# The last row of an output weight in two transfers by partitions, and fifteen tiny transfers behind it

## The chip, the cores and the metric

The kernel runs on one core of one Trainium2 chip. The metric is device time in microseconds (us) of one execution; the time before is the median of three runs. The trace is of one profiled execution, and its times are counted from the first instruction.

## What is computed

One decode step for two tokens of width 512, gated by a small MLP. Cut to what matters:

```python
x  = A_x                                      # (2, 1, 512)
xn = layernorm(x)
q  = (xn @ wq)                                # 32 heads of 128
p  = softmax(q . k_cache / sqrt(128))         # 2 x 32 heads x 8192 keys
o  = p @ v_cache                              # two caches of 268 MB each
s  = o.reshape(2, 1, 4096) @ wo               # wo: 4096 x 512, 8 MB
g  = silu(gelu(layernorm(xn) @ w1 + b1) @ w2 + b2)
return x + s * g
```

## The kernel before

The two caches are read in 32 steps of two heads each (`N = 32`); a step's keys are 8 MB, 64 KB on each of 128 partitions, and so are its values. Keys go to one of two buffers `kb`, values to the one buffer `vb`. In each step VectorE multiplies the keys by the query and sums (lines 555 and 562), ScalarE takes the exponentials (line 583), and TensorE (PE) weighs the values (line 606). The values of the last step go in two halves into a `kb` buffer, so that `vb` is free for `wo`.

All transfers are issued by SyncE (SP), in the order in which `load` (line 328) is called in the program, on one hardware queue. SP waits before an issue only until the destination's earlier users are done. A small planner (`Plan`) records every operation with what it reads and writes and puts the waits in: a transfer has a semaphore named by its third argument, which rises by 16 when the transfer has landed, and whoever reads its key waits for it. Transfers with the same name share one semaphore. A reader of several of them waits for the count of the last, that is for all.

The weight `wo` is viewed as 128 partitions by 32 rows `c` of 512 columns (`wo_r`), where partition p holds the 32 rows 32p to 32p + 31 of the matrix. It is loaded in seven pieces behind the last values: the rows `c` 0-15, 16-23, 24-28, 29, 30, and the last, 31, in two, columns 0-383 and 384-511. They are called wo0 to wo6 here, after their semaphores. The pieces are cut in lines 340 to 342 and loaded in lines 651 to 654:

```python
    for i, (a, e) in enumerate(((0, CUT), (CUT, D)), len(WO_PIECES) - 2):
        load(wo_sb[:, OC - 1, a:e], wo_r[:, OC - 1, a:e], f"wo{i}", [("wo", i)], over=["vb"])
```

When the last step's values are weighed and normalised (`on`), PE multiplies by `wo`, row by row as the pieces land: rows 0 to 23 in line 683, rows 24 to 28 in line 696, whose sum `acc` VectorE copies to `early` (line 698), and the rows 29, 30 and 31 in line 704, each in sixteen chunks of 32 columns (`chunks`), which is 32 instructions of PE, since each 32-bit matmul is two. Between row 30 and row 31 line 712 adds `early` in. `piece(c, n)` names the key of the piece that a chunk waits for. A scan on VectorE (line 718) multiplies by the gate and adds x, and SP issues the output (line 721), 112 rows of 256 bytes. The program ends when that has landed.

Of the kernel before, what the change touches and what calls it, by code (L numbers as in the profile page):

```python
# [21 lines left out]
class Plan:  # L22
# [18 lines left out]
    def op(self, eng, fn, r=(), w=(), over=(), it=None, loop=False, dma=None):  # L41


        o = Op()
        o.eng, o.fn, o.it, o.loop, o.dma, o.tell = eng, fn, it, loop, dma, False
        need = {}

        def after(d, war):
            if d.dma is None and dma is None and d.eng == eng and (eng == "pe" or war):
                return  # L50
            if d.dma is None:
                if need.get(d.eng) is None or need[d.eng].idx < d.idx:
                    need[d.eng] = d
            else:
                k = ("dma", d.dma)
                if need.get(k) is None or need[k].idx < d.idx:
                    need[k] = d

        for k in r:
            if k in self.writer:  # L60
                after(self.writer[k], False)
        for k in list(w) + list(over):
            if k in self.writer:
                after(self.writer[k], False)
            for d in self.readers.get(k, ()):
                after(d, True)
        clock = self.clock[eng]
        need = {k: d for k, d in need.items() if clock.get(k, 0) < d.idx}
        o.deps = [(k, d) for k, d in need.items()
                  if not any(e is not d and e.done.get(k, 0) >= d.idx for e in need.values())]  # L70
        for _, d in o.deps:
            for k, v in d.done.items():
                clock[k] = max(clock.get(k, 0), v)
        own = eng if dma is None else ("dma", dma)
        self.count[own] = o.idx = self.count.get(own, 0) + 1
        o.done = dict(clock)
        o.done[own] = o.idx
        for k in w:
            self.writer[k] = o
            self.readers[k] = []  # L80
        for k in r:
            if k not in w:
                self.readers.setdefault(k, []).append(o)
        self.ops.append(o)
# [80 lines left out]
def decode_kernel(nc, x, kc, vc, wq, wo, w1, b1, w2, b2, out):  # L165
# [20 lines left out]
    OC = DH // PH  # L186
    QS = 4
    CH = QT * QS
    CW = D // CH
# [11 lines left out]
    op = plan.op  # L201

    def pe(fn, r=(), w=(), it=None, loop=False):
        op("pe", fn, r, w, it=it, loop=loop)
# [10 lines left out]
    def sbuf(name, shape):  # L215
        return nc.alloc_sbuf_tensor(name, shape, F32).ap()

    def psum(name, shape):
        return nc.alloc_psum_tensor(name, shape, F32).ap()
# [5 lines left out]
    vb = sbuf("vb", [P, KP * DH])  # L225
# [3 lines left out]
    wo_sb = vb.rearrange("p (c n) -> p c n", c=OC)  # L229
# [9 lines left out]
    blk = sbuf("blk", [P, QT])  # L239

    pick = sbuf("pick", [B, P])

    b2w = sbuf("b2w", [P, R])

# [5 lines left out]
    res = sbuf("res", [P, CW, 2])  # L250
# [18 lines left out]
    onp = sbuf("onp", [P, LAST, 2 * CM - RM])  # L269
# [43 lines left out]
    wide = psum("wide", [P, D])  # L313
# [4 lines left out]
    def bank():  # L318
        i = turn[0] % 4
        turn[0] += 1  # L320
        return scratch[i], f"s{i}"
# [6 lines left out]
    def load(dst, src, sem, w, over=()):  # L328
        op("sp", lambda: nc.sync.dma_start(dst, src), (), w, over=over, dma=sem)
# [10 lines left out]
    WO_PIECES = (0, 16, 24, 29, 30, 31, 32)  # L340
    WIDE = WO_PIECES[-5]
    CUT = D - P


    load(w1_sb, w1.rearrange("(p c) f -> p c f", p=P), "w1", ["w1"])
# [54 lines left out]
    for c in range(QT):  # L400
        dve(lambda c=c: nc.vector.memset(b2w[R:R + 1, (QT * B + B) * c:(QT * B + B) * c + B], 1.0), ["b2w"], ["b2w"])
    dve(lambda: nc.vector.tensor_reduce(
        out=slot, in_=ident.rearrange("p (g r) -> p g r", r=R)[:, :, :CM].rearrange("p g (s b) -> p s g b", b=B),
# [103 lines left out]
    for i in range(NQ):  # L507
        for c in range(ND):
            wv = wq_sb[:, c, :].rearrange("p (h s d) -> p h s d", s=U, d=DH)
            a = (NQ - 1 - i) * B  # L510
# [8 lines left out]
    for k in range(N // NB):  # L519

        b, e = divmod(k, HH // NB)
        i, g = divmod(e, GQ)
        p, kp = bank()
        for s in range(U):
            a = R * (U * g + s) + B * i + b
# [124 lines left out]
    wo_r = wo.rearrange("(p c) n -> p c n", p=P)  # L650
    for i, (a, e) in enumerate(zip(WO_PIECES[:-1], WO_PIECES[1:-1])):
        load(wo_sb[:, a:e], wo_r[:, a:e], f"wo{i}", [("wo", i)], over=["vb"])
    for i, (a, e) in enumerate(((0, CUT), (CUT, D)), len(WO_PIECES) - 2):
        load(wo_sb[:, OC - 1, a:e], wo_r[:, OC - 1, a:e], f"wo{i}", [("wo", i)], over=["vb"])

    max_dve(N - 1)
    exps(N - 1)
# [19 lines left out]
    def piece(c, n=0):  # L677
        return ("wo", max(i for i, a in enumerate(WO_PIECES[:-1]) if a <= c) + int(c == OC - 1 and n >= CUT))

# [21 lines left out]
    def chunks(c, lo, hi):  # L701
        for q in range(lo, hi):
            g, sl = q % QT, q // QT
            pe(lambda c=c, q=q, g=g, sl=sl: matmul(
                sums[R * g:R * g + CM, :, 0], onp[:, c - (OC - LAST), CM - RM - RM * sl:2 * CM - RM - RM * sl],
                wo_sb[:, c, q * CW:(q + 1) * CW], start=(c == OC - LAST and sl == 0), stop=(c == OC - 1 and q >= CH - QT)),
               ["onp", piece(c, q * CW), "o4", "wide_x"], ["wide"])

    for c in range(OC - LAST, OC - 1):
        chunks(c, 0, CH)  # L710
    for g in range(QT):
        pe(lambda g=g: matmul(sums[R * g:R * g + CM, :, 0], to_own,
                              early[:, g * CW:(g + 1) * CW], start=False, stop=False),
           ["to_own", "early"], ["wide"])
    chunks(OC - 1, 0, CUT // CW)
    chunks(OC - 1, CUT // CW, CH)

    dve(lambda: nc.vector.tensor_tensor_scan(
        out=res.rearrange("p n k -> p (n k)"), data0=gate.rearrange("p n k -> p (n k)"), data1=wide[:, :2 * CW],
        initial=0.0, op0=ALU.mult, op1=ALU.add), ["wide", "wide_x"] + [("gate", j) for j in range(QT)], ["res"])  # L720
    op("sp", lambda: nc.sync.dma_start(out, res[:ROWS].rearrange("p n k -> p (n k)")), ["res"], dma="out")

    plan.emit(HEADS)

# [2 lines left out]
ROWS, COLS, TOKENS, BLOCK, SLOTS = 112, 64, 2, 32, 4  # L727
# [24 lines left out]
```

## Time and profile before

| | before |
|---|---|
| median of three runs | 1298.91 us (1298.90 to 1299.01) |
| span of the profiled execution, first to last instruction | 1297.6 us |
| time of the median outside that span | 1.3 us |
| DMA queue busy, share of 16 engines | 99.7% |
| read from HBM | 559.30 MB, 431 GB/s over the span |
| VectorE busy | 1138.0 us (88%) |
| PE busy | 407.6 us (31%) |

No time of the profiled execution other than its span is on record. A row such as `1267.28 26.18 DMA vb<-in_A_wo_dram` says at which time a piece of work began and how many us it took. A landing is the time of issue and the us to landing that the profile gives with it. "x32" is a count of instructions; PE's own work (PE) and its weight loads (PEld) have rows of their own, and a weight load begins where its matmul's waits are over. DMA share is the busy share of the 16 DMA engines in a stretch; a packet is one contiguous piece that an engine moves, or the write that reports a finished transfer.

### The profile page before, as it was taken

How to read it: one execution, taken by the hardware profiler on the slowest of the kernel's cores; microseconds unless marked ns; L12 is line 12 of the kernel's file. 1: busy time of each engine (PE TensorE's matmuls, PEld its weight loads, DVE VectorE, ACT ScalarE, POOL GpSimd, SP SyncE). 2: the span in 40 equal slices, each digit the busy share in tenths (PEclk: the TensorE clock that was granted, in tenths of full speed). 3: DMA queues.
4: the chain of work that ended last, by engine and by line, in shares of the span. 5: the costliest groups of instructions: out<-in, count | busy, mean ns of one | idle time of the engine just before them, and what ended most of it. 6: DMA issues, size and time to landing. Idle time of an engine off the chain costs nothing.

```text
span 1297.6 us, 6944 instructions
## 1 busy us (share of the span) xinstructions
PE 407.6 (31%) x2796; PEld 123.4 (10%) x2796; DVE 1138.0 (88%) x294; ACT 78.0 (6%) x250; POOL 1.4 (0%) x8
## 2 busy tenths in 40 slices
PE   5703333312333312333311333321333321233328
PEld 1100110000101000101100101100001100001103
DVE  3599999988889988889988888988888988888991
ACT  1200000000000000000000000000000000000000
POOL 0000000000000000000000000000000000000000
PEclk9856666556666656666656666656666655666658
DMA  9999999999999999999999999999999999999998
GB/s 404 445 425 440 428 432 438 426 444 424 434 438 424 446 424 440 430 426 444 426 438 430 430 440 426 444 424 434 438 424 446 424 432 438 424 446 426 425 433 372
DMA packets 11231, 559.42 MB, mean 431 GB/s; under 512 B 1364, under 2 KB 1620, under 8 KB 1880
## 3 DMA queue, kind: packets, MB, share of 16 engines
q1 hardware_dynamic: 11224, 559.33, 99.7%
q8 instruction: 4, 0.07, 0.0%
q14 instruction: 3, 0.02, 0.0%
HBM read 559.30 MB, written 0.03 MB: 431 GB/s over the span
## 4 chain that ended last, share of the span: by engine, by line
DMA 71%; PE 24%; DVE 3%; issue 1%; ACT 0%; SPq 0%; DVEq 0%
DMA vb<-in_A_v_cache_dram 68%; PE po L606 22%; DMA vb<-in_A_wo_dram 2%; DVE kb L555 1%; DVE sc L562 1%; PE s L433 1%; DMA vb<-in_A_x_dram 1%; PE po L513 1%; PE s L479 0%; PE s L435 0%; DVE vb L441 0%; DVE vb L380 0%; ACT L454 0%; PE acc L696 0%; PE s L486 0%
## 5 line engine op out<-in xcount | busy, mean ns | idle before, releaser
L555 DVE TENSOR_TENSOR kb<-kb,Q 128x8192 f32<-128x8192 f32 x64 | 555.5, 8681 | 99.6 <-DMA kb<-in_A_k_cache_dram 93.1
L562 DVE TENSOR_REDUCE sc<-kb 128x64 f32<-128x8192 f32 x64 | 552.3, 8666 | 0.0
L606 PE MATMUL po<-vb,PZ 128*8 128x512 f32 x1984 | 282.3, 733 | 286.1 <-DMA vb<-in_A_v_cache_dram 284.8
L578 PE MATMUL s<-nm,srow 1*128 1x2 f32 x64 | 18.6, 358 | 360.8 <-DVE nm L572 360.8
L606 PEld LDWEIGHTS po<-vb,PZ 128*8 128x8 f32 x1984 | 56.3, 103 | 485.9 <-issue 482.4
L569 PE MATMUL s<-ident,mx 128*1 128x128 f32 x32 | 11.8, 369 | 197.8 <-DVE mx L566 197.8
L578 PEld LDWEIGHTS s<-nm,srow 1*128 1x128 f32 x64 | 15.9, 306 | 370.1 <-DVE nm L572 370.1
L613 ACT COPY o<-po 128x512 f32<-128x512 f32 x32 | 18.8, 586 | 528.2 <-PE po L606 528.2
L579 ACT COPY bias<-s 128x2 f32<-128x2 f32 x32 | 5.1, 160 | 623.9 <-PE s L578 623.9
L615 PE MATMUL s<-mod,o 128*128 128x2 f32 x256 | 33.6, 253 | 22.1 <-ACT o L613 22.1
L615 PEld LDWEIGHTS s<-mod,o 128*128 128x128 f32 x256 | 31.1, 191 | 51.4 <-ACT o L613 51.4
L583 ACT ACTIVATE PZ<-sc,bias 64x128 f32<-64x128 f32 x64 | 25.5, 399 | 1.8
L569 PEld LDWEIGHTS s<-ident,mx 128*1 128x1 f32 x32 | 2.5, 79 | 201.4 <-DVE mx L566 170.8
L621 DVE TENSOR_TENSOR Z<-blk,s 128x8 f32 (+1 forms) x32 | 5.2, 163 | 13.3 <-PE s L615 13.3
L441 DVE COPY vb<-vb 2x384 f32<-2x384 f32 x4 | 1.8, 499 | 15.4 <-ACT vb L437 15.4
L433 PE MATMUL s<-vb 128*2 128x512 f32 (+1 forms) x24 | 12.1, 654 | 0.3 <-ACT vb L393 0.3
L583 ACT ACTIVATION_READ_ACCUMULATOR PZ<-sc,bias 64x1 f32 x64 | 11.8, 185 | 0.0
L566 DVE TENSOR_REDUCE mx<-sc 128x1 f32<-128x128 f32 x32 | 9.2, 286 | 1.1
L587 ACT ACTIVATE ZR<-half,rs 128x8 f32 (+1 forms) x32 | 9.6, 301 | 4.1
L606 PE MATMUL po<-kb,PZ 128*8 128x512 f32 x64 | 9.4, 754 | 1.4 <-ACT PZ L583 1.4
L572 DVE TENSOR_REDUCE nm<-s 1x2 f32<-1x128 f32 x32 | 8.7, 272 | 0.3 <-PE s L569 0.3
L688 DVE COPY wide<-x 128x32 f32<-128x32 f32 x1 | 0.2, 195 | 9.0 <-ACT o L686 9.0
(101 smaller groups left out, 90.3 us busy)
## 6 DMA issues: line engine op xcount, KB each, us to landing
kb<-in_A_k_cache_dram SPq DMA_DIRECT2D x4, 4096.0 KB, 42.9
kb<-in_A_v_cache_dram SPq DMA_DIRECT2D x2, 4096.0 KB, 40.9
vb<-in_B_w_dram SPq DMA_DIRECT2D x2, 2752.0 KB, 12.1
vb<-in_A_wo_dram SPq DMA_DIRECT2D x1, 4096.0 KB, 19.0
vb<-in_A_wo_dram SPq DMA_DIRECT2D x1, 2048.0 KB, 23.6
vb<-in_A_wo_dram SPq DMA_DIRECT2D x1, 1280.0 KB, 26.2
vb<-in_A_wo_dram SPq DMA_DIRECT2D x2, 256.0 KB, 26.3
vb<-in_A_v_cache_dram SPq DMA_DIRECT2D x31, 29.5
```

The source lines that it names most:

```text
L433: pe(lambda f=f, w=w, ph=ph, c=c: matmul(ph[:B, :w], yT[:, c, :], w1_sb[:, c, f:f + w], start=(c == 0), stop=False), ["yT", "w1"], [k])
L513: pe(lambda i=i, c=c, wv=wv, a=a, j=j, hd=hd: matmul(PO[R * j:R * j + NQ * B, :].rearrange("m (h d) -> m h d", d=DH), xnT[:, c, a:a + NQ * ...
L555: vector(n, n, lambda n: nc.vector.tensor_tensor(out=k, in0=k, in1=cols(Q, n * DH, DH).unsqueeze(1).to_broadcast([P, M, DH]), op=ALU.mult) ...
L562: vector(n, n, lambda n: nc.vector.tensor_reduce(out=SC[:, s * M:(s + 1) * M], in_=k, axis=AX.X, op=ALU.add), [("kb", i, s)], [("sc", s)])
L566: vector(n, n, lambda n: nc.vector.tensor_reduce(out=MX, in_=SC, axis=AX.X, op=ALU.max), [("sc", 0), ("sc", 1)], ["mx"])
L569: pe(lambda i: transpose(PM[:1, :P], MX, ident), ["mx", "ident"], ["s1"], it=n, loop=n > 0)
L578: pe(lambda i: matmul(PN[:, :U], srow, NM, start=True, stop=True), ["srow", "nm"], ["s2"], **one)
L583: act(lambda i, r=r, s=s: nc.scalar.activation(PZ[r, :, s, :], sc[r], AF.Exp, bias=BIAS[r, s:s + 1], scale=SCALE, accum_out=RS[r]), ["bias ...
L587: act(lambda i: nc.scalar.activation(cols(ZR, i * UP - UP, UP), half, AF.Copy, scale=RS), ["half"] + [("rs", s) for s in range(U)], [("ZR" ...
L606: pe(lambda i, t=t, j=j, v=v: matmul(PO[R * j:R * j + U * JW, :], PZ[:, t].rearrange("p s j -> p (s j)"), v[:, t * JW:(t + 1) * JW, :].rea ...
L613: act(lambda i: nc.scalar.copy(O4, PO), ["po"], ["o4"], **one)
L615: pe(lambda i, k=k: matmul(PT[:, :U], O4[:, k * DH:(k + 1) * DH], mod[:, k:U * JW:JW], start=(k == 0), stop=(k == JW - 1)), ["o4", "mod"], ...
```

## The change

The last row of `wo` is loaded by four transfers in place of two: for each of its two column ranges one for the partitions 0 to 119 and one, with a semaphore of its own, for the partitions 120 to 127. The chunks of row 31 wait for both transfers of their range. Behind them SP issues fifteen more transfers, of fifteen rows, fourteen, and so on down to one, each row 32 numbers (128 bytes) of row 0 of `wo`, into a tile `mark` that no instruction reads. They share the semaphore `mark`, and the output waits for all of them.

```diff
+    mark = sbuf("mark", [16, 512])
...
+    MAIN = 120
...
     for i, (a, e) in enumerate(((0, CUT), (CUT, D)), len(WO_PIECES) - 2):
-        load(wo_sb[:, OC - 1, a:e], wo_r[:, OC - 1, a:e], f"wo{i}", [("wo", i)], over=["vb"])
+        load(wo_sb[:MAIN, OC - 1, a:e], wo_r[:MAIN, OC - 1, a:e], f"wo{i}", [("wo", i)], over=["vb"])
+        load(wo_sb[MAIN:, OC - 1, a:e], wo_r[MAIN:, OC - 1, a:e], f"wo{i}r", [("wo", i, "rest")], over=["vb"])
+
+    for k in range(15, 0, -1):
+        load(mark[:k, 32 * k:32 * k + 32], wo_r[:k, 0, :32], "mark", [("mark", k)])
...
-               ["onp", piece(c, q * CW), "o4", "wide_x"], ["wide"])
+               ["onp", piece(c, q * CW), "o4", "wide_x"] + ([piece(c, q * CW) + ("rest",)] if c == OC - 1 else []),
+               ["wide"])
...
-    op("sp", lambda: nc.sync.dma_start(out, res[:ROWS].rearrange("p n k -> p (n k)")), ["res"], dma="out")
+    op("sp", lambda: nc.sync.dma_start(out, res[:ROWS].rearrange("p n k -> p (n k)")), ["res"] + [("mark", k) for k in range(1, 16)], dma="out")
```

## Rows read from the trace of the kernel before

**Rows 1.** The page: the DMA queue, what was read, and the chain that ended last.

```profile
q1 hardware_dynamic: 11224, 559.33, 99.7%
HBM read 559.30 MB, written 0.03 MB: 431 GB/s over the span
DMA 71%; PE 24%; DVE 3%; issue 1%; ACT 0%; SPq 0%; DVEq 0%
```

**Rows 2.** The chain that ended last, end of the span: start us, us, what.

```profile
1267.28 26.18 DMA vb<-in_A_wo_dram
1293.46 0.04 issue
1293.51 1.28 PE acc L696 x40
1294.78 0.56 PE wide L704 x64
1295.35 0.10 PE wide L712 x8
1295.44 0.34 PE wide L704 x32
1295.78 0.02 issue
1295.80 0.29 DVE res L718
```

**Rows 3.** Issues on SP in order of time: start us, us, engine, line, what.

```profile
1226.95 6.42 SPq L329 DMA_DIRECT2D kb<-in_A_v_cache_dram  x2
1266.44 3.44 SPq L329 DMA_DIRECT2D vb<-in_A_wo_dram  x7
...
1267.76 0.43 SPq L329 DMA_DIRECT2D vb<-in_A_wo_dram  x1
...
1268.60 0.33 SPq L329 DMA_DIRECT2D vb<-in_A_wo_dram  x1
...
1268.98 0.90 SPq L329 DMA_DIRECT2D vb<-in_A_wo_dram  x2
...
1269.45 0.43 SPq L329 DMA_DIRECT2D vb<-in_A_wo_dram  x1
```

**Rows 4.** DMA issues: KB each, us to landing (256.0 KB: wo3, then wo4).

```profile
kb<-in_A_v_cache_dram SPq DMA_DIRECT2D x2, 4096.0 KB, 40.9
...
vb<-in_A_wo_dram SPq DMA_DIRECT2D x1, 256.0 KB, 26.4
...
vb<-in_A_wo_dram SPq DMA_DIRECT2D x1, 256.0 KB, 26.2
...
vb<-in_A_wo_dram SPq DMA_DIRECT2D x1, 192.0 KB, 26.3
vb<-in_A_wo_dram SPq DMA_DIRECT2D x1, 64.0 KB, 26.0
out_dram<-res SPq DMA_DIRECT2D x1, 28.0 KB, 1.4
```

**Rows 5.** Line 704's weight loads begun by the stretch's end, in brackets (first: 1294.50).

```profile
1290.00:1294.84 4.84, 0.35 (x32) 1.00 0.83 320
1290.00:1294.87 4.87, 0.38 (x33) 1.00 0.82 318
1290.00:1295.13 5.13, 0.64 (x64) 1.00 0.78 302
1290.00:1295.29 5.29, 0.73 (x65) 1.00 0.76 293
1290.00:1295.44 5.44, 0.88 (x88) 1.00 0.74 285
1290.00:1295.47 5.47, 0.91 (x89) 1.00 0.74 283
```

**Rows 6.** The end in order of time: start us, us, engine, line, what [idle before].

```profile
1294.85 0.29 DVE L698 COPY early<-acc 128x128 f32<-128x128 f32 x1 [1.67 <-PE acc L696]
1295.19 0.12 PEld L712 LDWEIGHTS wide<-early,to_own 128*8 128x8 f32 x8
1296.12 0.35 SPq L721 DMA_DIRECT2D out_dram<-res  x1
```

**Rows 7.** Stretches of the end: busy time by engine, PE clock, DMA share, GB/s.

```profile
1293.50:1294.00 0.50, 0.49 (x20) 0.48 (x24) 0.00 (x0) 0.00 (x0) 0.00 (x0) 1.00 0.62 209
1294.00:1294.60 0.60, 0.60 (x32) 0.59 (x24) 0.00 (x0) 0.00 (x0) 0.00 (x0) 1.00 0.38 118
1294.60:1295.00 0.40, 0.40 (x54) 0.40 (x45) 0.15 (x1) 0.00 (x0) 0.00 (x0) 1.00 0.14 44
1295.00:1296.00 1.00, 0.71 (x77) 0.58 (x66) 0.34 (x2) 0.00 (x0) 0.00 (x0) 1.00 0.00 0
```

**Rows 8.** Packets of 1294.6 to 1295.0; left from 1294.9 on; from 1294.95 on.

```profile
DMA packets 31, 0.02 MB, mean 44 GB/s; under 512 B 5, under 2 KB 31, under 8 KB 31
...
DMA packets 134, 0.03 MB, mean 10 GB/s; under 512 B 130, under 2 KB 134, under 8 KB 134
...
DMA packets 130, 0.03 MB, mean 10 GB/s; under 512 B 129, under 2 KB 130, under 8 KB 130
```

**Rows 9.** Packets of 1296.5 to 1297.6 (the output); of the first 12 us.

```profile
DMA packets 128, 0.03 MB, mean 26 GB/s; under 512 B 128, under 2 KB 128, under 8 KB 128
...
DMA packets 210, 4.19 MB, mean 349 GB/s; under 512 B 18, under 2 KB 18, under 8 KB 20
```

**Rows 10.** What SP waited for before the output: us in total, times, longest.

```profile
SPq L721 <- DVE res L718: 26.2, 1, 26.2
```

## The prediction

> **What bounds the kernel now.** I read the page first. The one hardware DMA queue is busy for 99.7% of the time of its sixteen engines, and the chain that ended last is 71% DMA and 24% PE [rows 1]. For most of the span the kernel is a stream from HBM, and the change touches nothing of that stream: all it edits is issued after the last V chunk. So I read the end only.
>
> The chain of the end [rows 2] says: the third wo piece (wo2, columns 24 to 28) lands at 1293.46, then PE works without a gap until 1295.78, the scan takes 0.29, the output is issued. That is too coarse, because a PE that still drains a matmul counts as busy. I therefore put three views side by side. SP issues the seven wo pieces from 1266.44 on, the last at 1269.45 [rows 3]; with the time to landing of each [rows 4] the landings are wo2 1293.46, wo3 1267.76 + 26.4 = 1294.16, wo4 1268.60 + 26.2 = 1294.80, wo5 1268.98 + 26.3 = 1295.28, wo6 1269.45 + 26.0 = 1295.45. The counts of weight loads at line 704 that had begun by a given time [rows 5] show where PE waits: column 29 needs wo3 and begins at 1294.5, column 30 begins at 1294.87, after wo4, and has all 64 begun at 1295.13. The eight of line 712 follow at 1295.19, behind the copy of `acc` that ends at 1295.14 [rows 6]. The last row of wo, column 31, begins at 1295.29, right at the landing of wo5, and its last eight loads (columns 384 to 511, wo6) begin at 1295.47, right behind wo6. So the last row is in truth bound by the landing of wo5 and wo6, but hardly: 32 loads take (1295.13 - 1294.87) / 31 = 8.4 ns each at best, the eight of line 712 are issued by 1295.24, so without any wait column 31 could start at about 1295.245. The wait on wo5 is worth 0.045 us, and that on wo6 0.02 us, in which matmuls issued earlier still drain. Nothing else in the last 4 us can be given back by this change.
>
> Where do wo5 and wo6 lose time? The DMA share falls step by step, 0.62 over 1293.5 to 1294.0, 0.38 to 1294.6, 0.14 to 1295.0, then 0 [rows 7]. The engines thus finish one after another: what is left after 1293.5 is 0.62 x 0.5 + 0.38 x 0.6 + 0.14 x 0.4 = 0.59 us per engine in the mean, so a mean engine ends at about 1294.1 and the last at 1294.97. In the last stretch 31 packets are left, at 1294.95 two (130 less the 128 of the output, [rows 8, 9]).
>
> **The change part by part.** (a) *The last row by 120 and 8 partitions.* If the 120 partitions go to fifteen engines by eight rows, one engine loses its 16 packets of the last row (8 of 1,536 bytes, 8 of 512), and eight engines get one more row of each transfer. One packet in the tail takes 0.14 x 16 x 0.40 us / 31 = 29 ns [rows 7, 8], so the one engine saves about 16 x 29 = 0.46 us with its two completions some 0.5, and eight others get 2 rows and 2 completions, 0.12 us, more. If the spared engine is the single last one, wo5 and wo6 land earlier by what parts it from the next. At 1294.9 six packets with two completions among them are still left (134 and 130 less the output's 128, [rows 8, 9]), so a second engine was then still at work, less than 0.1 us ahead. Gain on the PE path: between 0 and the 0.065 us that PE waits at all. If a last engine is one of those that get a ninth row: a loss of up to 0.12 us. I take 0.
>
> The trace shows for 112 partitions sixteen completions beside the 112 rows (128 packets, the output) and at the start 18 packets below 512 bytes, which I read as 16 completions of w1 and 2 of x with its two rows [rows 9]; no transfer of 120 rows is in it. [...] No row here tells engines apart.
>
> (b) *Two more waits on PE*, before the first and the thirteenth chunk of column 31. Where column 30 waits for a piece that has landed, the step from load 32 to load 33 is 0.03 us against 0.01 between others [rows 5]: 0.02 us for each wait that is already satisfied, 0.04 us in all. It is on the path; behind it stand the last 32 matmuls, the scan and the output. Bounds 0 and 0.04; I take 0.04, which eats the gain of (a).
>
> (c) *Seventeen more DMA issues on SP.* Seven take 3.44 us [rows 3], 0.49 each; 24 take 11.8 us and end near 1278.2. SP has nothing else until the output: it waits 26.2 us there for the scan [rows 10], so 18 us of cover are left. Cost 0. If that cover were gone, each issue late would cost 0.47.
>
> (d) *The fifteen marks.* They lie behind the wo pieces on the queue, and the output (line 721) now waits for all of them as well as for the scan. Nothing but the output stands behind that wait on SP. Before, the output is issued at 1296.12 [rows 6]. A transfer's last packet precedes its landing by 1295.45 - 1294.97 = 0.48 us. [...] Lower price of a mark: two packets of 29 ns, 0.058 us. Upper price: the 0.17 us from the landing of wo5 to that of wo6, which holds eight rows and a completion. A mean engine with fifteen marks then ends at 1294.1 + 0.12 + 0.87 = 1295.09, landed 1295.57, hidden with 0.55 us to spare; the last engine, were it the one with fifteen, at 1295.96, landed 1296.44, 0.3 us too late. At the upper price these are 1297.25 and 1298.12: the output late by 1.1 and 2.0 us. A row of 128 bytes is nearer to a packet than to eight, so I take the lower price, and for the unknown place of the late engines half of the 0.3: 0.15 us.
>
> **Sum.** (a) 0, (b) +0.04, (c) 0, (d) +0.15: +0.19 us on the span of 1297.6. The median of the runs, 1298.91, lies 1.31 us above that span, and I keep this: 1298.91 + 0.19 = 1299.1. Differences of 0.2%, 2.6 us, are about what a measurement of this kernel can tell from no change, so this is no change.
>
> **The rivals.**
> *Marks in single file.* If each mark is begun only when the one before is written and acknowledged, each costs what the output needs from the end of its issue to landing, 1.4 - 0.35 = 1.05 us [rows 4, 6]. The engine with fifteen would end at 1294.2 + 15 x 1.05 = 1309.95, landed 1310.4, the output 14.3 us late: 1313.2, slower. It decides from 0.27 us a mark on ((1296.12 + 2.6 - 0.48 - 1294.2) / 15). Against it: wo5 and wo6 land only 0.17 us apart with eight rows between. Chance 3%. [...]
>
> *The 120 rows don't spread.* On eight engines (15 rows each) an engine gets 30 packets in place of 16: 14 x 29 ns = 0.4 us, at worst on the last one: 1299.5, still no change. On one engine: 240 packets x 29 ns = 7.0 us behind a mean engine's 1294.1 less its 0.5, landed near 1301.1 against 1295.45: +5.6, 1304.7, slower. For it speaks only that 120 is no power of two; against it that 112 rows made sixteen completions. Chances 5% and 2%.
>
> *The queue holds only so many transfers.* At most nine are in flight in the trace of before: seven wo pieces and two halves of the last V, issued from 1226.95 on with 40.9 us to landing [rows 3, 4]. If sixteen were the limit, the last marks would be issued only as wo5 and wo6 land, the last near 1296.2, landed near 1297.6: the output 1.5 us late, 1300.6, no change (4%). If nine or ten were, some ten marks would be issued after 1295.28 at 0.47 each, the last landed near 1301.4: 5.3 us late, 1304.4, slower (2%).
>
> *Faster.* All of the wait on the late engine is 0.065 us and the whole stretch from wo2's landing to the scan is 2.3 us; 0.2% would need more than this. Only a shift of the stream before, for which the diff has no cause, could give it: 3%.
>
> **How the numbers follow.** The forecast with its bounds (0 to 2.0 us late, or 0.07 earlier) holds 81%, together with the two rivals that stay within 0.2% (5% and 4%) 90%; slower 7%; faster 3%. The range goes from 1298.6 (the whole wait gained, and the 0.1 us by which the runs differ, twice) to 1301.0 (upper price of a mark on the last engine, 2.0 us).
>
> **What would show it.** In the changed profile: 24 wo and mark issues on SP, ended by about 1278; wo2 landing within 0.1 us of 27 us after the first wo issue; column 31 begun at 0.05 us or less behind line 712; the fifteen marks as 120 more packets below 512 bytes with 120 completions more, done within about 1 us of the last wo row; the output issued 0.03 us behind the scan, or up to 0.35 later, and then with SP's wait at line 721 put down to a mark. An output held by 2 us or more behind the scan, or column 31 a microsecond or more behind column 30, would make the prediction wrong.

## The result, and the profile after

| | before | after |
|---|---|---|
| median of the runs | 1298.91 us (20 runs, 1298.76 to 1299.22) | 1301.09 us (20 runs, 1300.80 to 1301.60) |
| ratio, 95% interval | | 1.0017 (1.0010 to 1.0023) |
| span of the profiled execution | 1297.6 us | 1299.6 us |
| scan begins | 1295.80 | 1296.67 |
| output issued | 1296.12 | 1298.10 |
| packets, of them below 512 bytes | 11231, 1364 | 11485, 1618 |

The median is 2.18 us later. That is within the 0.2% that I called "no change", yet no run of after is as fast as the slowest of before, and 1301.09 lies 0.09 above the range. The forecast of +0.19 us was wrong by a factor of eleven.

The chain that ended last, end of the span of the changed kernel (start us, us, what; line 704 of before is 710 here, 712 is 719, 718 is 725, 721 is 728, and 329 is 330):

```profile
1267.91 27.81 DMA vb<-in_A_wo_dram
1295.72 0.04 issue
1295.76 0.42 PE wide L710 x32
1296.18 0.10 PE wide L719 x8
1296.28 0.37 PE wide L710 x32
1296.65 0.02 issue
1296.67 0.29 DVE res L725
```

It answers to [rows 2]. Before, the last DMA of the chain was wo2, landed at 1293.46. Here it is wo4, row 30, issued at 1267.91 and landed at 1295.72; in before wo4 landed at 1294.80 [rows 3, 4]. So a piece that the change doesn't touch, queued ahead of all that it adds, is 0.92 us late, and the scan with it 0.87 us. This chain ends with the scan; the wait for the marks stands in SP's rows.

SP's issues in order of time (answering to [rows 3, 6]):

```profile
1265.75 5.80 SPq L330 DMA_DIRECT2D vb<-in_A_wo_dram  x9
1271.59 17.98 SPq L330 DMA_DIRECT2D mark<-in_A_wo_dram  x15
1298.10 0.34 SPq L728 DMA_DIRECT2D out_dram<-res  x1
```

and what SP waited for at the end (us in total, times, longest; answering to [rows 10]; line 107 is the planner's own wait, before the one that stands with the output in line 728):

```profile
SPq L107 <- DVE res L725: 7.4, 1, 7.4
SPq L728 <- DMA mark<-in_A_wo_dram: 1.1, 1, 1.1
```

The scan ends at 1296.96 and the output is issued at 1298.10: SP waits 1.1 us more, for the marks. The output is 1.98 us later than before, which is the whole difference of the spans. In order of time that is 0.87 us to the scan and 1.11 us more to the landing of the marks. But the output waits for the later of the two, and that is the marks alone: what makes them land late decides. Two things are late, then, and the prediction had priced both near nothing.

The DMA packets of 1293.0 to 1293.6, before and then after, show the first (packets and bytes; then the queue's packets, MB and busy share of the 16 engines):

```profile
DMA packets 172, 0.20 MB, mean 340 GB/s; under 512 B 21, under 2 KB 131, under 8 KB 172
q1 hardware_dynamic: 172, 0.20, 96.4%
```

```profile
DMA packets 141, 0.13 MB, mean 225 GB/s; under 512 B 48, under 2 KB 101, under 8 KB 141
q1 hardware_dynamic: 141, 0.13, 101.6%
```

The engines are busy in both, but move a third less after: 340 against 225 GB/s. (In such short stretches the share can pass 100%, so it is read here as "all busy" and no finer.) Is it the tiny marks that fill the time, or are the rows themselves slower? That needs each alone.

### The profile page after: what moved, and what is told of

Its sections match the earlier page's. It is cut to its first block, busy times and chain, and to the rows that moved or that the text cites. A ratio compares the mean times of both kernels' runs of the same rounds, so it can differ in the third digit from the quotient of the medians.

```text
span 1299.6 us, 6964 instructions
## 1 busy us (share of the span) xinstructions
PE 412.4 (32%) x2796; PEld 124.1 (10%) x2796; DVE 1138.0 (88%) x294; ACT 78.0 (6%) x250; POOL 1.4 (0%) x8
## 2 busy tenths in 40 slices
DMA packets 11485, 559.44 MB, mean 430 GB/s; under 512 B 1618, under 2 KB 1874, under 8 KB 2134
## 4 chain that ended last, share of the span: by engine, by line
DMA 70%; PE 25%; DVE 3%; issue 1%; ACT 0%; SPq 0%; DVEq 0%
DMA vb<-in_A_v_cache_dram 67%; PE po L608 22%; DMA vb<-in_A_wo_dram 2%; DVE kb L557 1%; DVE sc L564 1%; PE s L435 1%; DMA vb<-in_A_x_dram 1%; PE po L515 1%; PE s L481 0%; PE s L437 0%; SPq L330 0%; PE s L477 0%; DVE vb L443 0%; DVE vb L382 0%; PE s L488 0%
## 5 line engine op out<-in xcount | busy, mean ns | idle before, releaser
L608 PE MATMUL po<-vb,PZ 128*8 128x512 f32 x1984 | 288.2, 746 | 289.1 <-DMA vb<-in_A_v_cache_dram 287.8
## 6 DMA issues: line engine op xcount, KB each, us to landing
vb<-in_A_wo_dram SPq DMA_DIRECT2D x2, 256.0 KB, 27.8
```

What stands on the lines that cost most here:

```text
L608: pe(lambda i, t=t, j=j, v=v: matmul(PO[R * j:R * j + U * JW, :], PZ[:, t].rearrange("p s j -> p (s j)"), v[:, t * JW:(t + 1) * JW, :].rea ...
```

## The experiments

Theory M: the marks cost it all. Rival S: the uneven split makes the pieces late, and the marks only hold the output. Before was run again beside these kernels, with medians of 1298.88 to 1298.91 us. Most of the intervals below include 1, so the argument rests on the runs' ranges and on the rows: of e1 to e4, e6, e7 and e11 no run is as fast as the slowest of before (1299.11), while the runs of e5 and e12 overlap it.

**e1, the split alone.**

```diff
-    for k in range(15, 0, -1):
-        load(mark[:k, 32 * k:32 * k + 32], wo_r[:k, 0, :32], "mark", [("mark", k)])
...
-... ["res"] + [("mark", k) for k in range(1, 16)], dma="out")
+... ["res"], dma="out")
```

> The changed kernel without its fifteen marks: the last row of wo in 120 and 8 partitions, with the two more waits on PE, and the output waiting for the scan alone. In the changed kernel the scan begins 0.87 us later than before (1296.67 against 1295.80) and the output is issued 1.1 us after the scan's end. Theory M (the marks cost it all): time as before, 1298.9 within 0.2; wo4 lands near 1294.8, column 31 begins within 0.1 us of 1295.29, the output is issued 0.03 us behind the scan. Rival S (the uneven split makes the wo pieces late, the marks only hold the output): 1299.6 to 1299.9, column 31 begins 0.7 to 1 us later than before.

Measured: 1300.0 us (1299.52 to 1300.33), ratio 1.0008 (0.9998 to 1.0017); no run is as fast as the slowest of before (1299.10). The packets of the same stretch:

```profile
DMA packets 112, 0.13 MB, mean 214 GB/s; under 512 B 16, under 2 KB 77, under 8 KB 112
q1 hardware_dynamic: 112, 0.13, 97.3%
```

Without a single mark the engines move 214 GB/s. By these shares a packet takes about 0.973 x 16 x 0.6 us / 112 = 83 ns in the mean, against 0.964 x 16 x 0.6 / 172 = 54 ns before. In the half microsecond ahead, 1292.5 to 1293.0, the two still move nearly the same, before and then e1:

```profile
DMA packets 102, 0.19 MB, mean 376 GB/s; under 512 B 12, under 2 KB 37, under 8 KB 100
```

```profile
DMA packets 102, 0.18 MB, mean 359 GB/s; under 512 B 14, under 2 KB 48, under 8 KB 100
```

In e1 packets below 2 KB are 48 of 102 in this half microsecond and 77 of 112 in the stretch behind it (the last row's are of 512 and 1,536 bytes), and the rate falls from 359 to 214 GB/s; in before they are 37 of 102 and 131 of 172, and it falls from 376 to 340. Column 31 begins behind a wait:

```profile
1296.41 0.64 PE L707 MATMUL wide<-vb,onp 128*8 128x32 f32 x32 [0.23 <-DMA vb<-in_A_wo_dram]
1297.11 0.29 DVE L722 TENSOR_TENSOR_SCAN res<-gate,wide 128x64 f32<-128x64 f32 x1 [1.23 <-PE wide L707]
1297.43 0.34 SPq L725 DMA_DIRECT2D out_dram<-res  x1
```

The scan is 1.31 us late and the output follows it by 0.03 us, as before. Theory M falls; the split costs about 1.1 us by itself, 0.1 more than rival S had at most.

**e2, the marks alone**: the kernel before, with the marks and the output's wait for them.

```diff
+    for k in range(15, 0, -1):
+        load(mark[:k, 32 * k:32 * k + 32], wo_r[:k, 0, :32], "mark", [("mark", k)])
...
-... ["res"], dma="out")
+... ["res"] + [("mark", k) for k in range(1, 16)], dma="out")
```

> The kernel before with the fifteen marks and the output's wait for them, but with the last row of wo undivided. Theory M: as the changed kernel, 1300.8 to 1301.3, with wo4 landed 0.7 to 1 us later than before and the output held about 1.1 us. Rival S: wo4 lands as before, only the output is held: 1299.9 to 1300.2.

Measured: 1300.13 us (1299.77 to 1300.42), ratio 1.0009 (1.0000 to 1.0019).

```profile
1295.94 0.29 DVE L722 TENSOR_TENSOR_SCAN res<-gate,wide 128x64 f32<-128x64 f32 x1 [0.67 <-PE wide L708]
1297.42 0.34 SPq L725 DMA_DIRECT2D out_dram<-res  x1
```

The scan is only 0.14 us late; the output is held 1.2 us. Between 1293.0 and 1293.6 the engines move 327 GB/s in 248 packets. So the marks hardly slow the rows, as rival S has it. The two parts add up: 1.1 and 1.2 us alone, 2.2 together. They add up although the scan is not what the output waits for in the changed kernel: the marks stand behind the divided rows on the queue, and what had landed by 1297.42 here lands by 1298.10 there, 0.7 us later.

**e3, who sees the marks land?** The output waits for the scan alone, ScalarE for the marks.

```diff
-... ["res"] + [("mark", k) for k in range(1, 16)], dma="out")
+... ["res"], dma="out")
+    act(lambda: nc.scalar.copy(warm[:1], mark[:1, 32:33]), [("mark", k) for k in range(1, 16)], ["warm"])
```

> The changed kernel, but the output waits for the scan alone, and the wait for the fifteen marks stands on ScalarE, before a copy of one number at its very end; so ScalarE shows when the marks have landed. Theory M1 (the marks land 1.1 us after the scan): the output is issued 0.03 us behind the scan, ScalarE's copy begins near 1298.1, time 1299.8 to 1300.1, since the output lands then. Rival M2 (the marks have landed by about 1296.4, 0.5 us behind the last packet, and what held the output is SP itself): ScalarE's copy begins near 1296.4 and the output is issued late all the same, or the delay is gone and the time is the same 1299.8 to 1300.1; the start of the copy tells.

Measured: 1299.96 us (1299.73 to 1300.14), ratio 1.0008 (0.9998 to 1.0017).

```profile
1296.72 0.29 DVE L725 TENSOR_TENSOR_SCAN res<-gate,wide 128x64 f32<-128x64 f32 x1 [1.25 <-PE wide L710]
1297.04 0.34 SPq L728 DMA_DIRECT2D out_dram<-res  x1
1298.13 0.19 ACT L730 COPY warm<-mark 1x1 f32<-1x1 f32 x1 [5.08 <-DMA mark<-in_A_wo_dram]
```

M1 holds: ScalarE sees the marks land as late as SP did (1298.13 here, 1298.10 in the changed kernel), and an output that doesn't wait for them is issued 0.03 us behind the scan's end. Yet the last packet of the queue ahead of the output ended before 1296.0; this is 1296.0 to 1297.0:

```profile
DMA packets 0, 0.00 MB, mean 0 GB/s; under 512 B 0, under 2 KB 0, under 8 KB 0
```

The landing comes over 2 us behind it, where wo6's came 0.48 us behind its last packet in before.

**e4, all marks of one row**, fifteen rows in place of 120.

```diff
-        load(mark[:k, 32 * k:32 * k + 32], wo_r[:k, 0, :32], "mark", [("mark", k)])
+        load(mark[:1, 32 * k:32 * k + 32], wo_r[:1, 0, :32], "mark", [("mark", k)])
```

> The changed kernel with all fifteen marks of one row each, the same row: fifteen packets in place of 120. If the number of tiny packets on all engines together sets the cost (they slow each other and the late wo rows): almost nothing is left, 1299.0 to 1299.4. If the longest train of fifteen on one engine sets it: the output is held about 1.1 us as in the changed kernel, the scan begins as before: 1299.9 to 1300.3. If even the lateness of wo4 comes from the one engine or from SP's issues: 1300.8 to 1301.3.

Measured: 1300.8 us (1300.3 to 1301.0), ratio 1.0014 (1.0004 to 1.0023). The scan begins at 1296.63, the output is issued at 1297.97, 1.05 us behind the scan's end. So 105 rows fewer, and as many reports (11275 packets against 11485), bring the output forward by only 0.13 us, as it would be if the number of marks set the landing, not that of their rows. That the train is on one engine, as the expectation has it, no row shows. The lateness of the scan stays because the split is still in. My expectation for this case had forgotten that, and the time falls into the third range, whose cause e1 has ruled out: there the scan is late with no mark at all.

**e5, the eight-row transfers alone**: the last row whole, two transfers of eight rows more into an unread tile.

```diff
         load(wo_sb[:, OC - 1, a:e], wo_r[:, OC - 1, a:e], f"wo{i}", [("wo", i)], over=["vb"])
+        load(extra[120:, a:e], wo_r[120:, OC - 1, a:e], f"wo{i}r", [("extra", i)])
```

> The kernel before, its last row of wo whole, with two eight-row transfers (rows 120 to 127 of the same columns) into an unread tile, issued where the changed kernel issues its two; ScalarE waits for them with a copy at its very end, the output waits for the scan alone. Theory P (it is the packets of the 120-row transfers that hold the engines longer): wo2 lands as before, about 27.0 us after the first wo issue, the scan at most 0.2 us later than before, ScalarE's copy begins before 1296.2; 1298.9 to 1299.2. Rival Q (the eight-row transfers with their four reports in place of two cost it): the scan 0.7 to 1.1 us later, 1299.6 to 1300.1.

Measured: 1299.19 us (1299.05 to 1299.34), ratio 1.0003 (0.9992 to 1.0013). The scan begins at 1296.22, 0.42 us late, and ScalarE's copy at 1296.14. The rate between 1293.0 and 1293.6 is that of whole transfers:

```profile
DMA packets 170, 0.19 MB, mean 312 GB/s; under 512 B 25, under 2 KB 126, under 8 KB 170
```

About half of the 0.42 us has nothing to do with the edit. The product ahead of wo2, in order of time before and then in e5, waits for none of the pieces from wo2 on, and is 0.23 us late already:

```profile
1293.00 0.11 PEld L692 LDWEIGHTS acc<-o,mod 128*2 128x2 f32 x8 [1.64 <-ACT o L686]
```

```profile
1293.23 0.11 PEld L694 LDWEIGHTS acc<-o,mod 128*2 128x2 f32 x8 [1.64 <-ACT o L688]
```

This start differs from run to run (1293.21 in e1, 1292.91 in e7). Counted from it the scan of e5 is 0.19 us late, which is theory P. The loss of a third comes with the division (214 GB/s in e1), not with short transfers (312 here).

**e6, 112 and 16 partitions**, both multiples of sixteen.

```diff
-    MAIN = 120
+    MAIN = 112
```

> The last row of wo in 112 and 16 partitions in place of 120 and 8, no marks: both counts are multiples of sixteen. Theory P1 (the cost is that fifteen engines, not sixteen, take the long part, or that some engines get a row more): the scan at most 0.3 us later than before, 1298.9 to 1299.2. Theory P2 (any division of the 128 partitions costs it, since rows then go to other engines than in a transfer of 128): as the 120 and 8 alone, 1299.7 to 1300.2, with fewer than 45 packets per 0.2 us between 1293.0 and 1293.6 against 55 to 59 before.

Measured: 1299.91 us (1299.75 to 1300.03), ratio 1.0008 (0.9998 to 1.0018); the scan 1.03 us late. The stretch:

```profile
DMA packets 126, 0.14 MB, mean 232 GB/s; under 512 B 22, under 2 KB 100, under 8 KB 126
```

That is the time of P2: with 112 and 16, both multiples of sixteen, the median is within 0.09 us of that of 120 and 8 alone (e1). That rows then go to other engines, as P2 has it, no row shows.

**e7, other addresses in HBM**: the two parts of the last row read from rows 2 KB apart in place of 64 KB. The kernel so leaves out the last row's own product.

```diff
-        load(wo_sb[:MAIN, OC - 1, a:e], wo_r[:MAIN, OC - 1, a:e], ...
+        load(wo_sb[:MAIN, OC - 1, a:e], wo[:MAIN, a:e], ...
-        load(wo_sb[MAIN:, OC - 1, a:e], wo_r[MAIN:, OC - 1, a:e], ...
+        load(wo_sb[MAIN:, OC - 1, a:e], wo[MAIN:P, a:e], ...
```

> The 120 and 8 partitions alone, no marks, but the last row's data are read from rows that lie 2 KB apart in HBM in place of 64 KB (rows 0 to 127 of wo, so the last row's part of the output is left wrong). Theory R (the engines meet at one place of HBM, since row addresses 64 KB apart fall on other engines): the cost goes, the scan within 0.3 us of before, 1298.9 to 1299.2. Theory W (they meet on the way into SBUF, or the transfer's form costs it): as with the 120 and 8 alone, 1299.7 to 1300.2.

Measured: 1299.82 us (1299.61 to 1299.91), ratio 1.0007 (0.9997 to 1.0017); the scan 0.94 us late. The stretch:

```profile
DMA packets 108, 0.13 MB, mean 220 GB/s; under 512 B 14, under 2 KB 78, under 8 KB 108
```

Theory R falls: with the rows 2 KB apart in HBM the rate is 220 GB/s, with 64 KB 214 (e1).

**e11, 64 and 64 partitions.**

```diff
-    MAIN = 120
+    MAIN = 64
```

> The last row of wo in 64 and 64 partitions, no marks. Theory W (any division moves rows to other engines than a transfer of 128 and makes their packets long): the scan 0.7 us or more later than before, 1299.6 to 1300.1, fewer than 45 packets per 0.2 us between 1293.0 and 1293.6. If the cost were of counts that are no power of two or that leave engines unequal: only the two reports more, the scan 0.3 to 0.45 us late, 1299.2 to 1299.4.

Measured: 1299.97 us (1299.74 to 1300.17), ratio 1.0008 (0.9998 to 1.0018); the scan 1.14 us late.

```profile
DMA packets 119, 0.13 MB, mean 213 GB/s; under 512 B 23, under 2 KB 89, under 8 KB 119
q1 hardware_dynamic: 119, 0.13, 114.5%
```

Equal halves in powers of two cost the same as 120 and 8: 1299.97 us against 1300.0 (e1).

**e12, four transfers of all 128 partitions**, by columns: as many transfers as in e1, no division of the partitions.

```diff
-... in enumerate(((0, CUT), (CUT, D)), len(WO_PIECES) - 2):
+... in enumerate(((0, 192), (192, CUT), (CUT, 448), (448, D)), len(WO_PIECES) - 2):
...
-... + int(c == OC - 1 and n >= CUT))
+... + (int(n >= 192) + int(n >= CUT) + int(n >= 448)) * int(c == OC - 1))
```

> [...] Theory W and T together: the two reports more cost 0.2 us each on the late engine, the scan 0.3 to 0.45 us late, 1299.2 to 1299.4, and the packets between 1293.0 and 1293.6 as before, above 50 per 0.2 us. If the number of transfers is all of the cost of the 120 and 8: the scan about 1 us late, 1299.9.

Measured: 1299.05 us (1298.96 to 1299.39), ratio 1.0002 (0.9991 to 1.0012).

```profile
DMA packets 276, 0.19 MB, mean 313 GB/s; under 512 B 146, under 2 KB 230, under 8 KB 276
q1 hardware_dynamic: 276, 0.19, 98.3%
```

```profile
1295.99 0.29 DVE L718 TENSOR_TENSOR_SCAN res<-gate,wide 128x64 f32<-128x64 f32 x1 [0.79 <-PE wide L704]
```

The scan is 0.19 us late (0.11 counted from line 692), half of what I expected and a fifth of what a division costs, and the rate stays. e6 and e11 have the same four transfers, and e12 has more packets than they (11519 in all against 11263). It is the division of the partitions, not the number of transfers. Which engines move the rows is not shown, here or in e6 and e11.

**e8, e9, e10: one, eight and fifteen marks of one row**, behind the undivided last row. ScalarE waits for them, the output doesn't.

```diff
+    for k in range(1, 0, -1):     # e9: range(8, 0, -1); e10: range(15, 0, -1)
+        load(mark[:1, 32 * k:32 * k + 32], wo_r[:1, 0, :32], "mark", [("mark", k)])
...
+    act(lambda: nc.scalar.copy(warm[:1], mark[:1, 32:33]), [("mark", k) ...], ["warm"])
```

> The kernel before with one mark of one row behind the wo pieces; ScalarE waits for it with a copy at its very end, the output waits for the scan alone. With fifteen marks ScalarE's copy began near 1298.1, 2.2 us behind the last packet below 2 KB. Theory T (the reports of a train of transfers are served one after another, about 0.14 us each): the copy begins 0.1 to 0.4 us behind wo6's landing, near 1295.6 to 1295.9. Rival F (a tiny transfer behind the stream lands a fixed 2 us after its packet): near 1297.2. Time 1298.9 to 1299.1 under both, as the output lands at 1297.5.

> The kernel before with eight marks of one row each, ScalarE waiting for them at its very end. One mark had landed at 1294.25, the fifteen marks of fifteen rows down to one at about 1297.37, so 0.222 us for each more. Theory T (served one after another on one engine, a fixed price each): ScalarE's copy begins near 1295.85 (1294.29 and 7 x 0.222). If instead the delay sets in only from some length of the train on, or is fixed for more than one: before 1294.8 or after 1296.8.

> The same with fifteen marks of one row each. Theory T (the longest train on one engine sets the landing, not the number of packets on all): ScalarE's copy begins near 1297.4, as with the fifteen of fifteen rows down to one. If the 105 packets on other engines had a share: 1296.5 or earlier.

ScalarE's copy in the order of time of e8, e9 and e10:

```profile
1294.29 0.19 ACT L727 COPY warm<-mark 1x1 f32<-1x1 f32 x1 [1.27 <-DMA mark<-in_A_wo_dram]
```

```profile
1295.69 0.19 ACT L727 COPY warm<-mark 1x1 f32<-1x1 f32 x1 [2.67 <-DMA mark<-in_A_wo_dram]
```

```profile
1297.23 0.19 ACT L727 COPY warm<-mark 1x1 f32<-1x1 f32 x1 [4.07 <-DMA mark<-in_A_wo_dram]
```

A mark costs (1295.69 - 1294.29) / 7 = 0.20 us up to eight and (1297.23 - 1294.29) / 14 = 0.21 us up to fifteen. For e8 neither expectation was right: the single mark lands over 1 us ahead of wo6, whose last eight weight loads begin at 1295.47 in before [rows 5]. So there was no fixed 2 us behind the stream's end, and this transfer of one row landed while pieces ahead of it were still moving. The times are 1298.89 us for e8 (ratio 1.0000, 0.9990 to 1.0010), and single runs of 1298.97 and 1299.07 for e9 and e10. With 105 more rows and their reports (e2) the landing was 1297.4, hardly later, so it isn't the number of all reports. Whether the price goes by the engine or by the transfers of the queue isn't separated, since no row names the engine that moves a mark.

Where does this time lie? The packets of 1294.1 to 1294.3, in before and then in e10:

```profile
DMA packets 19, 0.02 MB, mean 100 GB/s; under 512 B 3, under 2 KB 16, under 8 KB 19
```

```profile
DMA packets 47, 0.02 MB, mean 106 GB/s; under 512 B 30, under 2 KB 42, under 8 KB 47
```

There are 27 packets below 512 bytes more, of the 30 that fifteen marks and their reports have. The train is thus nearly over by 1294.3, and ScalarE's copy begins 2.9 us behind it. In e9 the packets of the train show up between 1293.8 and 1293.9 (16 below 512 bytes from 1293.8 to 1294.0, against 3 in e8), and the copy begins 1.8 us behind them. The time of these trains is not spent on their packets but between them and the landing, and it grows from 1.8 us with eight marks to 2.9 us with fifteen. Counted in this way the last seven marks cost 0.16 us each.

## Why the prediction was wrong

**(a) failed, on the price of a packet.** I moved rows between engines at the 29 ns of a packet in the tail of before, which bounded the loss by 0.12 us, and took 0. That fifteen engines take the 120 rows by eight each was my assumption; no run shows which engine moves a row. What the runs show is the count of reports: 11485 - 11231 = 254 packets more are the 240 of the marks (11471 - 11231, e2) and 14 reports more, which is 15 + 8 in place of 16, twice; that a transfer of eight rows makes eight is seen in e5, where two of them add 32 packets, 16 rows and 16 reports (11263). And the price doesn't hold for a divided row. In e1 a packet of the stretch takes about 83 ns in place of 54. And pieces that I had treated as fixed land late: wo2's products begin at 1293.81 in place of 1293.51 in the changed kernel, and wo4 lands 0.92 us late. That the slow packets hold up engines still at earlier pieces fits this, but no row shows an engine by itself. Alone the division makes the scan 0.94 to 1.31 us late in four forms (e1, e6, e7, e11), 1.03 to 1.14 counted from the product ahead of wo2, and the medians 0.94 to 1.09 us longer. In the changed kernel it adds 1301.09 - 1300.13 = 0.96 us to the marks alone (e2). Two transfers more without a division make the scan 0.19 us late (e12). That a transfer of 120 rows makes fifteen reports and not sixteen is not the cause, since e6 and e11 cost the same, and their packets (11263) are as many as those of four transfers with sixteen reports each.

Why the packets of a divided row take longer, the runs don't settle. The distance of the rows in HBM is ruled out (e7: 220 GB/s with rows 2 KB apart). The way into SBUF and the form of the transfer were not tested apart, and no row names an engine. Equal halves don't avoid the loss: e11 is 1.07 us longer than before, for 256 KB.

**(b)** isn't separated from the rest: 0.04 us is below what (a) moved.

**(c) had the right cost and the wrong price.** The marks took 1.2 us each to issue (17.98 for fifteen) in place of 0.49, so the last was issued at 1289.57, not 1278.2, and the 18 us of cover were 7.4 in the end. Still hidden.

**(d) failed in the step from the last packet to the landing.** The wait was named rightly: the output waits for a train of marks. But I let a train end with its packets, at 0.058 us a mark, and land a fixed 0.48 us behind the last of them: 0.15 us in the sum. That one engine gets fifteen marks, a term of that sum, no run shows; in its place the runs show when one, eight and fifteen marks of one row have landed, by 1294.29, 1295.69 and 1297.23 (e8, e9, e10). Alone the marks of the changed kernel cost 1.22 us (e2). In e10 the packets of fifteen marks are nearly over by 1294.3 and the landing comes 2.9 us behind them. So the packets that I priced cost next to nothing, and the step that I took as fixed grew by 0.16 to 0.21 us with each mark (e8, e9, e10). What the landing waits for in that time no row shows. The upper price of 0.17 us was the better size, taken from the landings of wo5 and wo6. That it gave 1297.25 for a mean engine, where e10 shows 1297.2, is luck, since it put the time into the packets.

**The rivals.** "Marks in single file" was right that each mark has a price of its own, at a fifth of what it said, short of the 0.27 us a mark from which it would have passed 0.2%. It was wrong in the mechanism: 27 of e10's 30 packets lie within 0.2 us, so no mark waited for the landing of the one before. "The 120 rows don't spread" has the count against it, 15 reports for a transfer of 120 rows, though no row names their engines; and with sixteen reports for each transfer the medians are 1.03 (e6) and 1.07 us (e11) longer all the same. "The queue holds only so many" was right that the last marks are issued late (the issues ended at 1289.57), with no part in the time; that a limit of the queue does it was not shown. The range held the upper price of a mark, 2.0 us, but not the division's loss, and so fell 0.09 us short.

**The signs.** Three failed: the issues ended at 1289.57 in place of 1278, wo2's products began 28.1 us after the first wo issue in place of 27, and the output was held 1.1 us behind the scan in place of 0.35 at most. The two that were to make the prediction wrong, an output held by 2 us and column 31 a microsecond behind column 30, did not come (1.1 and 0.4 us): both asked for one large fault, and there were two of about 1 us.

## What to carry to other kernels

Leave a load to SBUF at all 128 partitions, and cut it by columns if it has to be cut: here, with the last 256 KB on the queue, a division of the partitions made the scan 0.9 to 1.3 us late, a cut by columns 0.2. Count transfers, not bytes, where something waits for a train of them: the busy time of their packets said little here of when they had landed (e10: nearly over by 1294.3, landed by 1297.2). And don't take the pieces ahead of a change on the queue as fixed: here wo4, ahead of all that was edited, landed 0.92 us late. Look also at what an end really waits for: the division cost here by way of the marks behind it, which landed 0.7 us later than in e2, not of the scan.

## What the hardware showed that I had not expected

- Each more transfer of one row of 128 bytes put off the landing of a train by 0.16 to 0.21 us (e8, e9, e10), though nearly all packets of fifteen of them are recorded within 0.2 us, 2.9 us before the copy that waits for them (e10).
- SP's issues were not equally fast: seven took 3.44 us before, the nine of after 5.80, and the marks 1.2 us each. It isn't the number of transfers alone: nine took 5.04 us in e11 and 9.50 in e12, whose last four have twice as many rows. The cause was not tested.
- With the engines busy in all of them (shares of 88% and more) the rate of 1293.0 to 1293.6 was 308 to 340 GB/s for undivided rows (before, e2, e5, e8, e9, e10, e12) and 208 to 232 for divided ones (after, e1, e3, e4, e6, e7, e11).
